# One attention product on 128 rows, a queue given to the scheduler, paired stores and a swapped copy in a fused attention and mixer kernel

## The chip, the cores and the metric

The kernel runs on one core of one Trainium2 chip. The metric is the device time of one execution in microseconds (us). The time before is 1947.83 us, the median of three runs (1947.3 to 1950.81).

## What is computed

Three layers in a row, on 8 batches of 576 tokens with 512 channels, all in 32-bit floats. Attention with keys and values averaged over eights, then a mixer with a low-rank product over tokens (U, V) and a two-layer network over channels, then a mixer that adds the real part of a two-dimensional Fourier transform, normalises, and applies a second two-layer network:

```python
k_p = k.reshape(B, H, Sp, pool, D).mean(axis=3)
v_p = v.reshape(B, H, Sp, pool, D).mean(axis=3)
scores = scale * np.matmul(q, k_p.transpose(0, 1, 3, 2))
scores = scores - np.max(scores, axis=-1, keepdims=True)
attn = np.exp(scores)
attn = attn / (np.sum(attn, axis=-1, keepdims=True) + 1e-09)
x = np.matmul(attn, v_p)                  # 8 heads side by side: 512 channels
u = x + (x.transpose(0, 2, 1) @ U @ V).transpose(0, 2, 1)
x = u + np.maximum(u @ w_ch1, 0.0) @ w_ch2
u = x + np.real(np.fft.fft(np.fft.fft(x, axis=1), axis=2))
un = (u - mu) / np.sqrt(var + 1e-06)
out = u + np.maximum(un @ w_ch1b, 0.0) @ w_ch2b
```

## The kernel before

Products run on TensorE in a reduced 32-bit format (`F32R`), with each operand split into a high and a low part, so that one product becomes three (high by high, high by low, low by high). Two of attention's products and its transposes run in plain 32-bit floats. The split takes a copy on ScalarE and a subtraction on VectorE or GpSimd (`split`, line 113).

**Attention** (`class Attn`, `tile_steps` from line 479) takes 128 tokens at a time: 5 tiles per batch, 40 in all. A tile's scores of 8 heads by 72 pooled keys make 576 columns. ScalarE exponentiates them head by head (line 503), TensorE transposes them (lines 507 to 509: four blocks of 128 columns, and one of 64 columns into `e1`), ScalarE copies the result into `e` (lines 512 and 513: a large copy of 512 columns and a small one of 64 partitions), and five products with `v` follow (lines 522 to 524). The fifth has 64 rows, for 576 is four and a half times 128. Tile `v` holds the averaged values with zeroes where a row belongs to another head. In the first batch three tiles are in flight, and three of its five tiles keep `e` in scratch space (`alt`); the other 37 tiles use the pool's `e`.

**Words.** The weights arrive as 64-bit floats and are converted to 32 bits by integer operations: `high` (a shift on VectorE, line 149, and an operation on ScalarE, line 150) and `bits` (two operations on VectorE, lines 154 and 155). `w_second` converts the second mixer's weights while attention is still running. Its second half takes 32 half words, each in one of two `cv` buffers, and stores each into the DRAM tensor `wd`; `w_swap` reads `wd` back much later.

**The last stage** (from line 1323, a loop over 14 blocks of 512 tokens, `seq`, 5 of the first mixer and 9 of the second; there are 13 changes of block). Each block runs 8 steps of 7 products (`product`, with weights combined beforehand, in the DRAM tensors `wc`), whose sums need fewer products than the plain way; between them stand the second layer's products of the step before (`st2_a`). A product is 12 matmuls. The combined weights come through a ring of four tiles `wr` of two products each (`ring_load`, line 971); 392 such loads of 512 KB run in the stage, and a tile is refilled one product after TensorE has finished with it. Around the products, four calls of `tick` per step advance the generators ("lanes") of the other work: attention's remaining tiles, the Fourier transform (`Dft`, loads `F` and `R` from `x1d`, stores to `u2d`), the preparation of the next block (`prep_a`, loads `ul`, statistics `mv`), `w_second`. At the end of a block the residuals `ur` are added and stored to `x1d` or `out` (line 1082), one per 128 tokens. In this stage attention runs in the way called `lean`: the small transpose goes into the right half of bank `h0`, whose left half is the target `u` of the products (`halves[0]`), and each step of a tile waits for its `tick`.

**What sets the order.** The program is written as a sequence; a scheduler orders each engine's instructions by a simulated timeline, except for engines named in a `manual_schedule` block, which keep the order of the program. ScalarE is named from the second group of blocks on, and in the last stage TensorE, VectorE and SyncE. SyncE issues nearly all DMAs, so its order is that of the transfers. The simulated timeline takes the place of times that the scheduler doesn't have; a queue whose head waits holds up all behind it. GpSimd is ordered by the scheduler throughout.

The lines that are touched:

```python
for c in range(4):
    nc.tensor.transpose(e0[:, c * 128:c * 128 + n], sf[:n, c * 128:c * 128 + 128], ident[:n, :n])
nc.tensor.transpose(e1[:64, :n], sf[:n, 512:S], ident[:n, :n])
...
k = TT[c][1]
mm(o[:n, h0 * D:(h0 + nh) * D], e[:k, c, :n], self.v[:k, v0:v0 + nh].rearrange("p h d -> p (h d)"), c == 0, c == 4)
```

Of the kernel before, what the change touches and what calls it, by code (L numbers as in the profile page):

```python
# [8 lines left out]
F32 = mybir.dt.float32  # L9
F32R = mybir.dt.float32r  # L10
I32 = mybir.dt.int32
ACTF = mybir.ActivationFunctionType
# [5 lines left out]
B, H, S, D = 8, 8, 576, 64  # L18
# [9 lines left out]
TT = [(0, 128), (128, 128), (256, 128), (384, 128), (512, 64)]  # L28
# [17 lines left out]
def kernel(  # L46
# [18 lines left out]
    nc = tc.nc  # L65
# [7 lines left out]
    ident = const.tile([128, 128], F32, name="ident")  # L73
# [6 lines left out]
    def scratch(i, w=1024, dt=F32):  # L80

        return wp.tile([128, w], dt, tag=f"w{i % 2}_{NF - 1 - i // 2}", name=f"scr{i}")
# [5 lines left out]
    wd = dram.tile([NF, 128, 512], F32, name="wd")  # L88
    wc = [dram.tile([7 * NPR, 128, 512], F32, name=f"wc{i}") for i in range(2)]

    def bank(tag):
        return ps_b.tile([128, 512], F32, tag=tag, name=tag)
# [9 lines left out]
    def at_tick(i):  # L102

        while state["lean"] and state["tick"] != i and not state["flush"]:
            yield

    def sub(eng, o, a, b):
        eng.tensor_tensor(out=o, in0=a, in1=b, op=ALU.subtract)  # L108
# [4 lines left out]
    def split(hi, lo, src, eng=None):  # L113
        nc.scalar.activation(out=hi, in_=src, func=ACTF.Copy)  # L114
        sub(eng or nc.vector, lo, src, hi.bitcast(F32))

    def mm(o, a, b, start, stop):
        nc.tensor.matmul(o, a, b, start=start, stop=stop, skip_group_check=True)  # L118
# [3 lines left out]
    def later(fn):  # L122

        if state["free"]:
            pend.append((state["clock"], fn))
        else:
            fn()
# [6 lines left out]
    def store(o, i):  # L134
        later(lambda: nc.sync.dma_start(out=o, in_=i))
# [6 lines left out]
    def pair(raw, n):  # L142
        v = raw.rearrange("p (n e) -> p n e", e=2)
        return v[:, 0:n, 0], v[:, 0:n, 1]

    def high(raw, n, t):

        lw, hw = pair(raw, n)
        nc.vector.tensor_scalar(out=t, in0=lw, scalar1=29, scalar2=None, op0=ALU.logical_shift_right)
        nc.scalar.activation(out=lw.bitcast(F32), in_=hw.bitcast(F32), func=ACTF.Abs, scale=F64_BIAS)  # L150

    def bits(raw, n, t):
        lw, hw = pair(raw, n)
        nc.vector.scalar_tensor_tensor(out=t, in0=hw, scalar=-0x80000000, in1=t, op0=ALU.bitwise_and, op1=ALU.bitwise_or)
        nc.vector.scalar_tensor_tensor(out=t, in0=lw, scalar=3, in1=t, op0=ALU.logical_shift_left, op1=ALU.bitwise_or)
        return t.bitcast(F32)
# [90 lines left out]
    def w_second(at):  # L247

        def load(src):
            raw = at.cv().bitcast(I32)  # L250
            nc.sync.dma_start(out=raw, in_=src.bitcast(I32))
            return raw

        def half(p, i, h):
            return w1b[2 * p + i][:, 256 * h:256 * h + 256]

        def raw_of(o):
            return o[:, 1].bitcast(F32)

        def put(o, n):  # L260
            split(o[:, 0], o[:, 1], raw_of(o), nc.gpsimd)
            store(wc[1][n], o.bitcast(F32).rearrange("p h x -> p (h x)"))

        n = [(p, i, h) for p in range(NPR) for i, h in ((0, 0), (1, 0), (1, 1), (0, 1))]
        ahead = [load(half(*n[0])), load(half(*n[1]))]
        at_n = [2]

        def word():
            raw = ahead.pop(0)
            o = at.wo()  # L270
            t = raw_of(o).bitcast(I32)
            high(raw, 256, t)
            yield
            bits(raw, 256, t)
            if at_n[0] < len(n):
                ahead.append(load(half(*n[at_n[0]])))
                at_n[0] += 1
            yield
            return o

        for p in range(NPR):
            z = 7 * p
            b11 = yield from word()
            b12 = yield from word()
            t1 = at.wo()
            sub(nc.vector, raw_of(t1), raw_of(b12), raw_of(b11))
            put(b11, z)
            yield
            b22 = yield from word()
            t2 = at.wo()  # L290
            sub(nc.vector, raw_of(t2), raw_of(b22), raw_of(t1))
            put(t1, z + 1)
            yield
            sub(nc.vector, raw_of(b12), raw_of(b22), raw_of(b12))
            put(b22, z + 4)
            yield
            put(b12, z + 3)
            b21 = yield from word()
            t4 = at.wo()
            sub(nc.vector, raw_of(t4), raw_of(b21), raw_of(t2))  # L300
            put(t2, z + 2)
            yield
            put(b21, z + 6)
            put(t4, z + 5)
            yield
        def load2(i):
            raw = at.wo().bitcast(I32).rearrange("p h x -> p (h x)")
            nc.sync.dma_start(out=raw, in_=w2b[i // 2][:, 256 * (i % 2):256 * (i % 2) + 256].bitcast(I32))
            return raw

        ahead = [load2(i) for i in range(3)]
        yield
        yield
        for i in range(2 * NF):
            raw = ahead.pop(0)
            t = at.cv()[:, 0:256].bitcast(I32)
            high(raw, 256, t)
            yield
            c = slice(256 * (i % 2), 256 * (i % 2) + 256)
            store(wd[i // 2][:, c], bits(raw, 256, t))  # L320
            if i + 3 < 2 * NF:
                ahead.append(load2(i + 3))
            yield
# [9 lines left out]
    class Attn:  # L333
        def __init__(self, c):
            p1 = self.p = c.enter_context(tc.tile_pool(name="at", bufs=1, side="right"))
            self.k = p1.tile([128, NPAIR, 2 * SP], F32, name="k")
            self.v = p1.tile([128, 12, D], F32, name="v")
            self.s = p1.tile([128, S], F32, name="s")
            self.mask = p1.tile([128, 12], F32, name="vmask")
            self.ust = p1.tile([128, 5, 4, RANK], F32R, name="ust")  # L340
            self.usf = scratch(21)[:, 0:20 * RANK].rearrange("p (t g r) -> p t g r", t=5, g=4)
            self.vst = p1.tile([128, S], F32R, name="vst")
            self.kp = {}
            self.hu = {}
            self.q = {}
            self.raw = {}
            self.mixing = False
            self.done = {}
            self.xq = [scratch(12 + t) for t in range(5)]
            self.x0 = [z[:, 0:512] for z in self.xq]  # L350

        def setup(self):
            nc.vector.memset(self.k, 0.0)
            nc.gpsimd.memset(self.usf[:, :, 1, :], 0.0)
            nc.gpsimd.dma_start(out=self.mask, in_=vmask)

        def tmp(self):
# [114 lines left out]
        def tile_steps(self, b, t, alt=0, before=None):  # L472
            p1 = self.p

            n = 128

            def banks():
                return [bank("soh"[alt] + i) for i in "01"]
# [3 lines left out]
            for p in range(NPAIR):  # L482
                o = sc[p // 2][:n, (p % 2) * 144:(p % 2) * 144 + 144]
# [5 lines left out]
            sf = scratch(3 + alt) if alt else self.s  # L489
# [3 lines left out]
            for i in range(2):  # L493
                h = slice(4 * i, 4 * i + 4)
# [9 lines left out]
            yield  # L504
            yield from at_tick(3)
            e0, e1 = (bank("s0"), halves[0][:, 256:512]) if state["lean"] else banks()
            for c in range(4):
                nc.tensor.transpose(e0[:, c * 128:c * 128 + n], sf[:n, c * 128:c * 128 + 128], ident[:n, :n])
            nc.tensor.transpose(e1[:64, :n], sf[:n, 512:S], ident[:n, :n])
            e = scratch(4 + 2 * alt, 640) if alt else p1.tile([128, 640], F32, tag="e", name="e")  # L510
            e = e.rearrange("p (c k) -> p c k", c=5)
            nc.scalar.activation(out=e[:, 0:4, :n], in_=e0.rearrange("p (c k) -> p c k", c=4)[:, :, :n], func=ACTF.Copy)
            nc.scalar.activation(out=e[:64, 4, :n], in_=e1[:64, :n], func=ACTF.Copy)
            nc.vector.tensor_scalar(out=sm[:n], in0=sm[:n], scalar1=1e-9, scalar2=None, op0=ALU.add)
            nc.vector.reciprocal(out=sm[:n], in_=sm[:n])
            yield
# [3 lines left out]
                    before()  # L520
            o = bank("soh"[alt] + "0")
            for c, (v0, h0, nh) in enumerate(VSLOT):
                k = TT[c][1]
                mm(o[:n, h0 * D:(h0 + nh) * D], e[:k, c, :n], self.v[:k, v0:v0 + nh].rearrange("p h d -> p (h d)"), c == 0, c == 4)
            if b == 0:
                xf = self.x0[t]
            else:
# [622 lines left out]
    at = Attn(abx)  # L1150
# [171 lines left out]

    prev, rows, low = None, None, None
    chain = ExitStack()
    chain.enter_context(tc.manual_schedule(engines={mybir.EngineType.PE, mybir.EngineType.DVE, mybir.EngineType.SP}))
    for k in range(len(seq)):
        begun = k + 1 == len(seq)
        for p in range(NPR):
            x = ops[k]
            n = 7 * (NPR * k + p)  # L1330
# [4 lines left out]
            h0, h1 = halves[0], bank("h1")  # L1335
# [153 lines left out]
```

## Time and profile before

| | before |
|---|---|
| median of three runs | 1947.83 us |
| the profiled execution | 1953.33 us |
| its span, first to last instruction | 1951.5 us |
| mean granted TensorE clock | 0.980 |
| TensorE matmuls busy | 1849.3 us (95%), 11500 instructions |
| TensorE weight loads busy | 1646.2 us (84%) |
| VectorE busy | 1070.6 us (55%) |
| ScalarE busy | 719.8 us (37%) |
| GpSimd busy | 197.2 us (10%) |
| moved by DMA | 423.78 MB, mean 217 GB/s |

The table comes from the page of the profiled execution. PE is TensorE's matmuls, PEld its weight loads, DVE VectorE, ACT ScalarE, POOL GpSimd, and SP SyncE; a "q" behind the name marks an instruction of the engine's queue, such as the issue of a DMA. L118 is a line of the kernel; as it belongs to the helper that issues every matmul, the names of the tiles tell products apart. Matmuls are pipelined and their ends are modelled, so starts tell more than durations. A group's mean is in nanoseconds, all else in microseconds. A wait is put down to the event that ended it.

### The profile page before, as it was taken

How to read it: one execution, taken by the hardware profiler on the slowest of the kernel's cores; microseconds unless marked ns; L12 is line 12 of the kernel's file. 1: busy time of each engine (PE TensorE's matmuls, PEld its weight loads, DVE VectorE, ACT ScalarE, POOL GpSimd, SP SyncE). 2: the span in 40 equal slices, each digit the busy share in tenths (PEclk: the TensorE clock that was granted, in tenths of full speed). 3: DMA queues.
4: the chain of work that ended last, by engine and by line, in shares of the span. 5: the costliest groups of instructions: out<-in, count | busy, mean ns of one | idle time of the engine just before them, and what ended most of it. 6: DMA issues, size and time to landing. Idle time of an engine off the chain costs nothing. (4 is left out here: it accounts for less than half of the span.)

```text
span 1951.5 us, 32024 instructions
## 1 busy us (share of the span) xinstructions
PE 1849.3 (95%) x11500; PEld 1646.2 (84%) x11500; DVE 1070.6 (55%) x2457; ACT 719.8 (37%) x2201; POOL 197.2 (10%) x335
## 2 busy tenths in 40 slices
PE   5789999999998998999999999999999999999999
PEld 4678888888887887898998888899989999999998
DVE  7884466656665554445455665555545544444332
ACT  5552444444454443333333433333323333232321
POOL 3440122221200000000001000100010000000000
PEclk8799999999999999999999999999999999999999
DMA  9654474757576677867576867676767666757664
GB/s 362 224 167 133 141 217 149 234 165 243 182 257 229 217 238 248 282 209 242 191 255 221 270 226 238 199 242 220 221 206 245 210 226 190 244 165 238 192 197 151
DMA packets 265278, 423.78 MB, mean 217 GB/s; under 512 B 45792, under 2 KB 76608, under 8 KB 265120
## 3 DMA queue, kind: packets, MB, share of 16 engines
q1 hardware_dynamic: 264192, 418.34, 66.3%
q0 software_dynamic: 928, 3.40, 0.5%
q8 instruction: 91, 1.49, 0.3%
q14 instruction: 67, 0.55, 0.1%
HBM read 342.09 MB, written 79.56 MB: 216 GB/s over the span
## 5 line engine op out<-in xcount | busy, mean ns | idle before, releaser
L118 PE MATMUL h<-x,wr 128*128 128x256 f32 x4704 | 646.4, 285 | 27.3 <-DMA wr<-wc 14.3
L118 PEld LDWEIGHTS h<-x,wr 128*128 128x128 f32 x4704 | 618.5, 192 | 62.1 <-issue 10.6
L118 PE MATMUL o<-w,hh 128*128 128x512 f32 x1312 | 371.7, 400 | 8.6 <-ACT hh L1026 5.9
L118 PEld LDWEIGHTS o<-w,hh 128*128 128x128 f32 x1312 | 228.3, 190 | 44.5 <-ACT hh L1026 9.1
L118 PEld LDWEIGHTS h<-utx,w 128*128 128x128 f32 x1536 | 203.4, 195 | 21.5 <-DVE hl L1027 9.6
L118 PE MATMUL h<-utx,w 128*128 128x256 f32 x1536 | 212.8, 290 | 9.1 <-DVE hl L1027 5.8
L111 DVE TENSOR_TENSOR side<-h,side 128x256 f32<-128x256 f32 x224 | 124.0, 553 | 172.9 <-PE h L118 171.6
L118 PE MATMUL o<-w,hl 128*128 128x512 f32 x656 | 212.0, 397 | 0.0
L1302 ACT ACTIVATE hh<-side 128x256 fp32r<-128x256 f32 x224 | 117.0, 522 | 146.6 <-DVE side L111 130.6
L1302 ACT ACTIVATE hh<-h 128x256 fp32r<-128x256 f32 x112 | 43.2, 386 | 300.1 <-PE h L118 298.5
L1308 DVE SCALAR_TENSOR_TENSOR hl<-h,hh 128x256 fp32r<-128x256 f32 x112 | 47.5, 424 | 181.1 <-ACT hh L1302 181.1
L1308 DVE SCALAR_TENSOR_TENSOR hl<-side,hh 128x256 fp32r<-128x256 f32 x224 | 123.4, 551 | 28.3 <-ACT hh L1302 28.2
L118 PEld LDWEIGHTS o<-w,hl 128*128 128x128 f32 x656 | 119.9, 190 | 22.0 <-DVE hl L1027 0.5
L118 PE MATMUL m<-w,hh 128*128 128x512 f32 x464 | 128.7, 398 | 0.0
L118 PE MATMUL hu<-w,hh 128*128 128x512 f32 x448 | 124.3, 400 | 0.0
L503 ACT ACTIVATE s<-s,mx 128x72 f32<-128x72 f32 x296 | 90.4, 329 | 43.4 <-DVE mx L496 43.1
L108 POOL TENSOR_TENSOR wo<-wo 128x256 fp32r<-128x256 f32 x88 | 68.9, 799 | 305.8 <-ACT wo L114 236.4
L108 DVE TENSOR_TENSOR x<-ul,x 128x256 fp32r<-128x256 f32 x182 | 70.1, 421 | 47.3 <-ACT x L114 47.2
L118 PEld LDWEIGHTS m<-w,hh 128*128 128x128 f32 x464 | 81.1, 192 | 11.0
L1349 ACT ACTIVATE side<-h 128x256 f32<-128x256 f32 x112 | 42.9, 383 | 120.3 <-PE h L118 119.9
L118 PEld LDWEIGHTS hu<-w,hh 128*128 128x128 f32 x448 | 78.2, 192 | 10.3
L118 PEld LDWEIGHTS s<-v,e 128*128 128x128 f32 (+1 forms) x370 | 59.5, 195 | 18.9 <-issue 9.0
(250 smaller groups left out, 2392.3 us busy)
## 6 DMA issues: line engine op xcount, KB each, us to landing
wr<-wc SPq DMA_DIRECT2D x392, 512.0 KB
wc<-wo SPq DMA_DIRECT2D x88, 256.0 KB
x<-x SPq DMA_DIRECT2D x56, 256.0 KB
ur<-ud SPq DMA_DIRECT2D x36, 256.0 KB
x1d<-ur SPq DMA_DIRECT2D x36, 256.0 KB
ul<-u2d SPq DMA_DIRECT2D x36, 256.0 KB
ur<-u2d SPq DMA_DIRECT2D x36, 256.0 KB
out<-ur SPq DMA_DIRECT2D x36, 256.0 KB
```

Source lines behind the costliest of these rows:

```text
L108: eng.tensor_tensor(out=o, in0=a, in1=b, op=ALU.subtract)
L111: eng.tensor_tensor(out=o, in0=a, in1=b, op=ALU.add)
L118: nc.tensor.matmul(o, a, b, start=start, stop=stop, skip_group_check=True)
L503: nc.scalar.activation(out=s[:n, a], in_=v[:, k], func=ACTF.Exp, bias=mx[:n, a:a + 1], accum_out=sm[:n, a:a + 1])
L1302: nc.scalar.activation(out=hh[:, i], in_=c, func=ACTF.Relu)
L1308: nc.vector.scalar_tensor_tensor(out=hl[:, i], in0=c, scalar=0.0, in1=hh[:, i].bitcast(F32), op0=ALU.max, op1=ALU.subtract)
L1349: nc.scalar.activation(out=sb, in_=v, func=ACTF.Copy)
```

## The change

It has four parts. The fifth product with `v` reads all 128 partitions of `e` and `v`; the upper halves are set to zero, once for the lasting tiles (`e` now lasts for the whole of attention) and per tile for scratch. The small transpose and the small copy stand ahead of the large ones. In `w_second` two converted half words share one `cv` buffer and leave with one store. In the last stage SyncE is no longer among the engines that keep the program's order.

```diff
@@ w_second
         for i in range(2 * NF):
             raw = ahead.pop(0)
-            t = at.cv()[:, 0:256].bitcast(I32)
+            if i % 2 == 0:
+                w = at.cv()
+            t = w[:, 256 * (i % 2):256 * (i % 2) + 256].bitcast(I32)
             high(raw, 256, t)
             yield
-            c = slice(256 * (i % 2), 256 * (i % 2) + 256)
-            store(wd[i // 2][:, c], bits(raw, 256, t))
+            bits(raw, 256, t)
+            if i % 2:
+                store(wd[i // 2], w)
@@ Attn.__init__
+            self.e = p1.tile([128, 640], F32, name="e")
@@ Attn.setup
+            nc.gpsimd.memset(self.v[64:128, 11], 0.0)
+            nc.gpsimd.memset(self.e[64:128, 512:640], 0.0)
@@ Attn.tile_steps
+            nc.tensor.transpose(e1[:64, :n], sf[:n, 512:S], ident[:n, :n])
             for c in range(4):
                 nc.tensor.transpose(e0[:, c * 128:c * 128 + n], sf[:n, c * 128:c * 128 + 128], ident[:n, :n])
-            nc.tensor.transpose(e1[:64, :n], sf[:n, 512:S], ident[:n, :n])
-            e = scratch(4 + 2 * alt, 640) if alt else p1.tile([128, 640], F32, tag="e", name="e")
+            e = scratch(4 + 2 * alt, 640) if alt else self.e
+            if alt:
+                nc.gpsimd.memset(e[64:128, 512:640], 0.0)
             e = e.rearrange("p (c k) -> p c k", c=5)
+            nc.scalar.activation(out=e[:64, 4, :n], in_=e1[:64, :n], func=ACTF.Copy)
             nc.scalar.activation(out=e[:, 0:4, :n], in_=e0.rearrange("p (c k) -> p c k", c=4)[:, :, :n], func=ACTF.Copy)
-            nc.scalar.activation(out=e[:64, 4, :n], in_=e1[:64, :n], func=ACTF.Copy)
...
-                k = TT[c][1]
-                mm(o[:n, h0 * D:(h0 + nh) * D], e[:k, c, :n], self.v[:k, v0:v0 + nh].rearrange("p h d -> p (h d)"), c == 0, c == 4)
+                mm(o[:n, h0 * D:(h0 + nh) * D], e[:, c, :n], self.v[:, v0:v0 + nh].rearrange("p h d -> p (h d)"), c == 0, c == 4)
@@ the last stage
-    chain.enter_context(tc.manual_schedule(engines={mybir.EngineType.PE, mybir.EngineType.DVE, mybir.EngineType.SP}))
+    chain.enter_context(tc.manual_schedule(engines={mybir.EngineType.PE, mybir.EngineType.DVE}))
```

## Rows read from the trace of the kernel before

**Rows 1.** Table of stretches: length, busy us (instructions) by engine, TensorE clock, DMA share, GB/s.

```profile
500.00:600.00 100.00, 92.20 (x587) 81.22 (x587) 65.20 (x162) 50.81 (x197) 14.43 (x21) 0.99 0.75 245
...
1600.00:1700.00 100.00, 100.00 (x632) 90.18 (x631) 47.52 (x114) 30.06 (x76) 4.05 (x6) 1.00 0.67 220
```

**Rows 2.** List of waits, TensorE: who, for whom, us in total, times, longest.

```profile
PE h L118 <- DMA wr<-wc: 14.3, 8, 2.7
...
PE h L923 <- DVE side L111: 6.5, 3, 5.7
...
PE h L118 <- ACT e L513: 6.2, 7, 1.8
...
PE h L118 <- DVE mv L892: 4.4, 1, 4.4
```

**Rows 3.** Groups by form: names, shapes, count | busy, mean ns | idle before, releasers.

```profile
L508 PE MATMUL s<-ident,s 128*128 128x128 f32 x148 | 26.6, 274 | 1.6 <-ACT s L503 1.3
...
L118 PEld LDWEIGHTS s<-v,e 64*128 64x128 f32 x74 | 11.1, 188 | 8.9 <-issue 8.6 <-ACT hh L1026 0.3
```

**Rows 4.** Timeline, 640 to 650 us: start, length, engine, instruction, count [idle before, releaser].

```profile
640.82 1.59 PE L118 MATMUL h<-x,wr 128*128 128x256 f32 x12
...
647.16 1.29 PEld L118 LDWEIGHTS s<-v,e 128*128 128x128 f32 x8
...
648.67 0.29 PEld L118 LDWEIGHTS s<-v,e 64*128 64x128 f32 x2 [0.23 <-issue]
...
649.03 1.48 PEld L118 LDWEIGHTS h<-x,wr 128*128 128x128 f32 x12
649.03 1.69 PE L118 MATMUL h<-x,wr 128*128 128x256 f32 x12
```

**Rows 5.** Timeline, the copies of one tile in the last stage, around 661 us.

```profile
660.81 0.58 ACT L512 ACTIVATE e<-s 128x512 f32<-128x512 f32 x1
...
661.28 0.26 ACT L513 ACTIVATE e<-h 64x128 f32<-64x128 f32 x1
...
661.60 0.62 PE L118 MATMUL h<-x,wr 128*128 128x256 f32 x3 [1.79 <-ACT e L513]
```

**Rows 6.** Timeline of GpSimd, a memset at the start.

```profile
3.44 0.26 POOL L354 MEMSET scr<- 128x160 f32 x1
```

**Rows 7.** Timeline around two stalls of VectorE, 598 and 740 us.

```profile
598.18 0.42 PE L509 MATMUL h<-ident,s 128*64 128x128 f32 x1 [3.93 <-DVE hl L1308]
...
732.17 0.42 SPq L135 DMA_DIRECT2D wd<-cv  x1
...
740.19 0.29 DVE L149 TENSOR_SCALAR cv<-wo 128x256 int32<-128x256 int32 x1 [7.02 <-DMA wd<-cv]
...
742.66 1.11 PE L923 MATMUL h<-ident,ul 128*128 128x128 f32 x4 [5.73 <-DVE side L111]
```

**Rows 8.** Table of stretches of 4 us around the two stalls.

```profile
734.00:738.00 4.00, 2.93 (x19) 2.29 (x17) 0.00 (x0) 0.00 (x0) 0.00 (x0) 1.00 1.02 313
742.00:746.00 4.00, 3.34 (x13) 3.15 (x14) 2.08 (x5) 2.13 (x5) 0.00 (x0) 0.50 0.68 233
...
598.00:602.00 4.00, 3.08 (x12) 2.38 (x13) 2.03 (x6) 1.75 (x4) 0.00 (x0) 0.50 0.66 242
```

**Rows 9.** List of waits of SyncE's queue, whole kernel.

```profile
SPq L971 <- PE h L118: 614.7, 278, 7.1
SPq L1082 <- DVE ur L111: 95.3, 36, 12.4
```

**Rows 10.** Timeline of SyncE and TensorE around a change of block, 1098 to 1125 us.

```profile
1098.40 4.84 SPq L971 DMA_DIRECT2D wr<-wc  x3
...
1113.18 0.38 SPq L971 DMA_DIRECT2D wr<-wc  x1
...
1124.61 1.67 PE L118 MATMUL h<-x,wr 128*128 128x256 f32 x12 [2.64 <-DMA wr<-wc]
```

**Rows 11.** Timeline of SyncE, four residual loads at a change of block.

```profile
799.19 4.63 SPq L1062 DMA_DIRECT2D ur<-ud  x4
```

## Prediction

> **What bounds the kernel now.** I read the table of stretches first. The reader is to see the TensorE column: in the late stretch it is busy for all of the 100 us, while in the attention stretch 7.8 us of 100 are missing [rows 1]. So TensorE's queue is the bound throughout, and a change can win in two ways only: by taking time off TensorE's own instructions, or by closing one of the gaps in it. Then I read the list of waits for TensorE. In the last stage, the chain of seven products, the gaps have few owners: a ring load of combined weights that lands late (14.3 us in 8 waits), VectorE's `side` (6.5 us), the small copy L513 (6.2 us in 7 waits), and the statistics `mv` (4.4 us in one) [rows 2]. Late in that stage there is nothing left to close [rows 1]. The profiled execution took 1953.33 us with a span of 1951.5; the median of the three runs is 1947.83, 5.5 us less. I make the sum in the profile's microseconds and take it off the median, because no term below is larger than a few tens of us and 0.3% of it is nothing.
>
> **Part 1, the fifth product on 128 rows.** Before, the last of five products of a tile of attention reads 64 partitions, with two weight loads of 64 rows. They cost no more than full ones (188 ns mean), but they have an idle stretch ahead of them: 8.9 us over 74 loads, 8.6 of it held by nothing that the profile shows [rows 3]. In the timeline it is plain: eight full weight loads end at 647.16 + 1.29 = 648.45, the 64-row pair begins at 648.67 after 0.23 us of idle weight path, ends at 648.96, and the next product's loads begin at 649.03, 0.07 later [rows 4]. All other weight loads there follow without a gap, so full-row loads should too. Saved per tile: 0.23 + 0.07 = 0.30 us. The lower end is 0.23 (entering alone); the upper is 0.40, since the next product's twelve matmuls then also took 1.69 us against 1.59 elsewhere [rows 4]. I take 0.30, because both gaps stand in the row and the 0.10 may be the modelled ends. There are 40 tiles (37 in `e`, 3 in scratch): 12 us, ends 9.2 and 16. The Trainium skill, "TensorEngine Tiling (Array Packing)", section Key Properties, says that a change of tiling mode drains TensorE; the row agrees for the way in, with 0.23 us, and by that rule, which holds for the way in and out, the sum is the 12 us, and by the way in alone 9.2. Not all of it reaches the end: the attention stretch has 7.8% of gaps that other engines set, and time saved ahead of such a gap only widens it. I count three quarters: **9 us**.
>
> What it adds: zeroes for the upper halves of `e` and `v`, two memsets at the start and three for the scratch tiles of the first batch, all on GpSimd. A larger one there took 0.26 us [rows 6]. Nothing waits for them but the fifth product of a tile, which comes after four others and two copies, so I cost them at nothing; without that cover they are at most 5 x 0.26 = 1.3 us.
>
> **Part 2, small transpose and small copy first.** In the last stage of attention (`lean`) the small transpose shares a bank with TensorE's next product. So that product waits for L513, which stands behind the large copy L512: they start at 660.81 and 661.28, and TensorE starts at 661.60 after 1.79 us [rows 5]. Swapped, L513 starts where L512 starts now, 0.47 us earlier, and TensorE with it. Seven tiles: 7 x 0.47 = 3.3 us; TensorE waits in all seven [rows 2], so I take **3 us**. What is late next is ScalarE's queue ahead of L512, which keeps the rest of the 1.79. Two waits are moved ahead of work that did not wait for them: the four large transposes (26.6 us over 37 tiles, 0.72 us each [rows 3]) now queue behind the small one, which needs the last exponential and, in `lean`, VectorE's `hl` (3.93 us at 598.18 [rows 7]). Where that wait binds, up to 0.72 us of transposes follow it instead of preceding it; in `lean` TensorE then stands waiting for ScalarE anyway, which covers it. Without that cover it is 7 x 0.72 = 5 us. Ends: 3.3 gained, 2 lost.
>
> **Part 3, two converted words in one buffer and one store.** `w_second` puts one converted half word into each of two `cv` buffers, and VectorE's order is fixed by hand. So when a `cv` store has not landed, the next conversion stops VectorE, and all behind it: at 740.19 after 7.02 us, for a store of which SyncE shows the issue at 732.17; TensorE's transposes at 742.66, which wait for `side` behind it, lost 5.73 us. At 598.18 the same happened with 3.93 us, behind `hl` [rows 7]. After each, the granted clock stood at 0.50 for the next stretch of 4 us [rows 8], the lower of its two levels (1.2 of 2.4 GHz), which costs up to 2.0 us each. With two words per buffer, a conversion waits for the store of the pair before the last, so two to three words old instead of one to two. The two stalls then go: 5.7 + 3.9 + 4.0 = 13.6 us. What is late next is the ring: the DMA engines are full in 734 to 738 (share 1.02 [rows 8]), so a TensorE that doesn't stop there may soon wait for weights. I count two thirds: **9 us**; ends 0 and 13.6. Sixteen stores fewer save SyncE 16 x 0.42 us (the issue at 732.17), which I cost at nothing, since SyncE stands waiting for most of that stage [rows 9].
>
> **Part 4, SyncE in the scheduler's order.** In the last stage SyncE issues in program order and stands behind whatever comes first: 614.7 us behind TensorE for ring loads, 95.3 us behind VectorE for the residual stores, the longest 12.4 [rows 9]. The first costs nothing by itself. The second does: at each end of a block SyncE stops at loads and stores of the block's end, and then issues everything at once. Around 1100 us the ring loads end at 1098.40 + 4.84, the next is issued at 1113.18, ten microseconds later, and at 1124.61 TensorE waits 2.64 us for one [rows 10]. A queue ordered by a simulated time puts what is ready ahead of what is not; moved past each other are the ring loads (392), the block loads `ul`, `ur`, `F`, `R`, and the stores `x1d`, `u2d` and `out`. At most it closes the waits for ring loads and for `mv`: 14.3 + 4.4 = 18.7 us [rows 2]. No row shows how well the simulated times fit the chip here, so the other end is a loss (the last rival). I take half, nearest to the rows in which SyncE demonstrably stood still: **9 us**.
>
> Sum: 9 + 3 + 9 + 9 = 30; 1947.8 - 30 = **1918 us**.
>
> **Rivals.**
> 1. *SyncE's new order gains nothing.* For it: full DMA engines (1.02), not only the order, delay ring loads. Against: the ten idle microseconds [rows 10]. Then 9 + 3 + 9 = 21 are left: 1927 us.
> 2. *The stall on `cv` is replaced by a wait for ring loads* at the same places, since the transfers' backlog stays. For it: the same 1.02. Against: four ring tiles stand ahead. Then 9 + 3 + 9 = 21: also 1927 us.
> 3. *Nothing reaches the end*: the saved matmul time and the closed stalls are taken up by ScalarE and VectorE in the stage where attention runs. For it: the 7.8 us of gaps in the attention stretch; against: TensorE is busy for the other 92. About 1946 us.
> 4. *Slower: block loads overtake ring loads.* The simulated order lets block loads out as soon as their buffers are free, so that they lie ahead of the ring loads that TensorE needs next. The place is each of the 13 changes of block in the last stage. The trace has one such case in little: four `ur` loads held SyncE for 4.63 us at 799.19 [rows 11], and a wait for the ring followed, of the longest kind (2.7 [rows 2]). With two such waits at each of 13 changes, 13 x 5.4 = 70 us, less the 14 that are there: 56 lost, 21 gained by the rest, 1947.8 + 35 = 1983 us. It decides from (21 + 14) / 13 = 2.7 us at each change, one such wait. Against it: late changes show none, so there is slack in the ring. The Trainium skill, "DMA: Bandwidth & Descriptors", section Queues, rings and completion order, says that on each DMA engine descriptors are consumed in ring order; by that rule what SyncE issues early is also served early, which is this rival. The wait behind the four `ur` loads agrees.
>
> **How the numbers follow.** The forecast has 0.45, rivals 1 and 2 0.20 and 0.12, rival 3 0.10, rival 4 0.13. The largest gain is 16 + 3.3 + 13.6 + 18.7 = 52 us, 1896; the three middle rivals lie below 1948. The range 1897 to 1948 leaves out rival 4 and a little on either side. A measurement of this kernel tells about 0.2% (3.9 us) from no change. Faster takes the forecast, rivals 1 and 2 and a fifth of rival 3: 0.79. Same takes most of rival 3: 0.08. Slower is rival 4: 0.13.
>
> **What would show it.** Part 1: no idle ahead of the fifth product's weight loads, and no 64-row form. Part 2: no wait of TensorE for L513, and less before the next product. Part 3: no DVE wait for `wd` stores; the gaps at 598 and 742 gone and the clock at 1.0 there. Part 4: fewer waits of TensorE for `wr`, ring loads issued at even distances across a change of block. The prediction is wrong if ring waits grow in number at the changes of block, or if the stretches before the last stage, where the simulation orders all queues anew, come out longer by more than part 1 gives.

## The result, and the profile after

The changed kernel takes 1916.13 us, the median of four runs (1915.26 to 1920.1), beside 1949.32 us (1947.3 to 1952.44) for the kernel before. The ratio is 0.9832, with an interval of 0.9812 to 0.9853, so about 33 us are gone. The forecast was 1918 us. The sum of 30 us was nearly right, yet three of its four terms were not: done alone, the parts give about 9, 0, 3 and 24 where the prediction had 9, 3, 9 and 9.

From the page of the changed kernel, its span and the busy time of TensorE (matmuls and weight loads), VectorE, ScalarE and GpSimd; the execution took 1916.54 us:

```profile
span 1914.8 us, 31951 instructions
...
PE 1827.1 (95%) x11500; PEld 1638.3 (86%) x11500; DVE 1074.9 (56%) x2457; ACT 717.8 (37%) x2201; POOL 194.5 (10%) x340
```

The span is 36.7 us shorter. TensorE's busy time falls from 1849.3 to 1827.1 us, so 22.2 us are matmuls that took less time, and the other 14.5 are gaps that closed. The prediction thought mostly of gaps.

The table of stretches of the changed kernel, with the columns of [rows 1]; the first two lines answer to [rows 1], the third to the last line of [rows 8]:

```profile
500.00:600.00 100.00, 92.03 (x597) 82.30 (x596) 67.61 (x165) 51.71 (x200) 14.28 (x21) 0.99 0.72 238
1600.00:1700.00 100.00, 100.00 (x634) 90.18 (x633) 43.02 (x105) 29.74 (x74) 2.58 (x4) 1.00 0.70 201
598.00:602.00 4.00, 3.80 (x18) 3.22 (x17) 1.65 (x5) 2.47 (x7) 0.00 (x0) 0.57 1.07 378
```

Nothing moved in the attention stretch or late in the last stage. What changed lies in the last stage's first 840 us: its last wait of over 1 us ended at 1419 us before. The granted clock at 598 us is still low (0.57, where the prediction wanted 1.0), but TensorE is busy for 3.80 us of the 4 where it was busy for 3.08.

The list of waits of the changed kernel, for TensorE and then for VectorE (for whom, us in total, times, longest):

```profile
PE h L118 <- DMA wr<-wc: 4.1, 4, 2.0
PE h L513 <- DVE hl L1315: 2.6, 2, 2.0
...
PE h L118 <- DVE side L111: 2.2, 4, 0.8
...
PE h L118 <- ACT e L520: 1.6, 2, 0.9
...
PE h L930 <- DVE side L111: 0.5, 2, 0.3
...
DVE cv L149 <- DMA wd<-cv: 0.6, 1, 0.6
```

All owners of [rows 2] have shrunk: the ring from 14.3 to 4.1 us, the small copy (now L520) from 6.2 to 1.6, the wait of 4.4 us for `mv` is gone, and the transposes' wait for `side` (now L930) fell from 6.5 to 0.5. The products' own wait for `side` grew a little, to 2.2 us in short waits (1.2 before). For `hl` TensorE still waits 2.6 us at the place of the stall at 598 us, where it waited 3.9.

To compare kernels by stage, two lines were read from the view of each tile: the first product of attention's stage (`h<-utx`) and the first of the last stage (`h<-x,wr`), with shortest, median and longest duration in ns, first start and last start. For the changed kernel:

```profile
L118 PE MATMUL h<-utx,w x1536: 274/283/582, 71.6 to 583.3; 128*128 128x256 f32 x192
L118 PE MATMUL h<-x,wr x4704: 274/283/583, 585.3 to 1903.9; 128*128 128x256 f32 x196
```

and for the kernel before:

```profile
L118 PE MATMUL h<-utx,w x1536: 274/283/582, 68.9 to 580.2; 128*128 128x256 f32 x192
L118 PE MATMUL h<-x,wr x4704: 274/283/583, 582.1 to 1940.7; 128*128 128x256 f32 x196
```

So the start stage lasts to 71.6 us (68.9 before), attention's stage 585.3 - 71.6 = 513.7 us (513.2), and the last stage, to the end of the span, 1914.8 - 585.3 = 1329.5 us (1369.4). The whole gain, 39.9 us, lies in the last stage, and 2.7 us of it were lost again at the start. The table of stretches tells gaps from slower matmuls in that stage; the first line is the kernel before, the second the changed one:

```profile
582.10:1951.50 1369.40, 1326.24 (x8335) 1192.21 (x8333) 688.96 (x1638) 448.57 (x1199) 57.43 (x166) 0.99 0.69 222
585.30:1914.80 1329.50, 1311.71 (x8335) 1184.67 (x8333) 687.78 (x1637) 446.76 (x1199) 58.28 (x166) 1.00 0.72 229
```

TensorE is idle for 43.2 us of it before and for 17.8 after, so 25.4 of the 39.9 us are gaps and 14.5 are matmul time. All kernels side by side, times in us:

| kernel | median | ratio to before, interval | start | attention | last stage |
|---|---|---|---|---|---|
| before | 1949.32 | | 68.9 | 513.2 | 1369.4 |
| changed | 1916.13 | 0.9832, 0.9812 to 0.9853 | 71.6 | 513.7 | 1329.5 |
| e1_rows_alone | 1941.75 | 0.9956, 0.9940 to 0.9972 | 68.2 | 512.2 | 1366.1 |
| e2_small_first | 1950.27 | 1.0009, 0.9992 to 1.0026 | 71.4 | 517.9 | 1363.6 |
| e3_pairs_alone | 1945.88 | 0.9984, 0.9963 to 1.0005 | 68.7 | 520.0 | 1357.9 |
| e4_sync_alone | 1928.49 | 0.9879, 0.9845 to 0.9913 | 68.7 | 517.9 | 1338.8 |
| e5_all_but_rows | 1921.90 | 0.9857, 0.9835 to 0.9879 | 70.7 | 518.1 | 1330.6 |
| e6_all_but_small_first | 1917.21 | 0.9830, 0.9807 to 0.9854 | 69.2 | 510.4 | 1333.2 |
| e7_all_but_pairs | 1918.37 | 0.9834, 0.9806 to 0.9861 | 71.7 | 510.9 | 1336.3 |
| e8_store_later | 1949.10 | 1.0004, 0.9987 to 1.0021 | 68.8 | 518.9 | 1368.9 |
| e9_small_first_late_only | 1915.42 | 0.9826, 0.9801 to 0.9851 | 68.5 | 514.3 | 1329.5 |
| e10_changed_again | 1919.04 | 0.9844, 0.9817 to 0.9871 | 72.1 | 515.1 | 1333.7 |
| e11_stores_elsewhere | 1949.54 | 1.0005, 0.9983 to 1.0026 | 69.1 | 510.6 | 1368.0 |
| e12_loads_elsewhere | 1941.29 | 0.9958, 0.9941 to 0.9975 | 68.8 | 513.2 | 1356.1 |

The stages come from one profiled execution each; those of e1, e2 and e8 are the longest of their ten runs. In before, e4, e8, e11 and e12, TensorE, VectorE and ScalarE execute the same instructions in the same order, and yet the middle column runs from 510.6 to 518.9. It can't be used for differences of a few us. The last column is steadier, but the changed kernel itself has 1329.5 and, taken again in e10, 1333.7. The verdicts rest on the medians.

### The profile page after: what moved, and what is told of

It is laid out like the page before. It is cut to its first block, busy times and chain, and to the rows that moved or that the text cites. A ratio compares the mean times of both kernels' runs of the same rounds, so it can differ in the third digit from the quotient of the medians.

```text
span 1914.8 us, 31951 instructions
## 1 busy us (share of the span) xinstructions
PE 1827.1 (95%) x11500; PEld 1638.3 (86%) x11500; DVE 1074.9 (56%) x2457; ACT 717.8 (37%) x2201; POOL 194.5 (10%) x340
## 3 DMA queue, kind: packets, MB, share of 16 engines
q1 hardware_dynamic: 261888, 418.33, 68.7%
## 5 line engine op out<-in xcount | busy, mean ns | idle before, releaser
L108 POOL TENSOR_TENSOR wo<-wo 128x256 fp32r<-128x256 f32 x88 | 68.5, 795 | 299.6 <-ACT wo L114 242.9
L118 PEld LDWEIGHTS m<-w,hh 128*128 128x128 f32 x464 | 80.2, 190 | 10.8
L118 PE MATMUL m<-w,hl 128*128 128x512 f32 x232 | 72.6, 391 | 0.0
```

## The experiments

The theory was the prediction's: four independent gains. The rivals were those of the prediction. First each part was done alone.

### Part 1 alone

```diff
...
-            e = scratch(4 + 2 * alt, 640) if alt else p1.tile([128, 640], F32, tag="e", name="e")
+            e = scratch(4 + 2 * alt, 640) if alt else self.e
...
-                mm(o[...], e[:k, c, :n], self.v[:k, v0:v0 + nh]..., c == 0, c == 4)
+                mm(o[...], e[:, c, :n], self.v[:, v0:v0 + nh]..., c == 0, c == 4)
```

> The kernel before with part 1 alone: the fifth product on 128 rows, with its zeroes. All expect the idle weight path ahead of that product to be gone, 0.30 us or a little more per tile in the starts. The prediction (three quarters of 12 us reach the end): 9 us faster. Rival (the attention stage before the last one is held by what the other engines hand over, so that the time saved there widens the next gap): only the 8 tiles of the last stage count, 8 x 0.34 = 2.7 us faster, and the start of the last stage stays within 2 us of 582.

It measured 1 - 0.9956 = 0.44%, 8.6 us (5.5 to 11.7), so the rival's 2.7 us fall. Its other sign, a start of the last stage within 2 us of 582, did come (580.4), but in a column that spreads by more than that: in which stage the 8.6 us were saved isn't shown. In the groups by form the fifth product, 16.2 us in 74 matmuls at 300 ns before, has become (count | busy, mean ns | idle before):

```profile
L118 PE MATMUL s<-v,e 128*128 128x64 f32 x74 | 12.6, 253 | 0.0
```

The timeline of the changed kernel, to be held beside [rows 4] (start, length, engine, instruction, count):

```profile
643.80 1.61 PEld L118 LDWEIGHTS s<-v,e 128*128 128x128 f32 x10
644.02 1.53 PE L118 MATMUL s<-v,e 128*128 128x128 f32 x10
...
645.33 1.50 PEld L118 LDWEIGHTS h<-x,wr 128*128 128x128 f32 x12
```

All ten weight loads now stand in one row, without idle time ahead of the last two. From the first of them to the first load of the next product it is 645.33 - 643.80 = 1.53 us, where [rows 4] have 649.03 - 647.16 = 1.87. The switch to 64 rows and back cost 0.34 us per tile. In e1, with part 1 alone, the median of the same distance is 1.54 us over 22 tiles that can be read in both, beside 1.88 in the kernel before.

### Part 2 alone

```diff
+            nc.tensor.transpose(e1[:64, :n], sf[:n, 512:S], ident[:n, :n])
             for c in range(4):
                 nc.tensor.transpose(e0[...], ...)
-            nc.tensor.transpose(e1[:64, :n], sf[:n, 512:S], ident[:n, :n])
...
+            nc.scalar.activation(out=e[:64, 4, :n], in_=e1[:64, :n], func=ACTF.Copy)
             nc.scalar.activation(out=e[:, 0:4, :n], ...)
-            nc.scalar.activation(out=e[:64, 4, :n], in_=e1[:64, :n], func=ACTF.Copy)
```

> The kernel before with part 2 alone: the small transpose and the small copy first. The prediction: 3 us faster, all of it in the seven tiles of the last stage, where TensorE's wait for the small copy shrinks by 0.47 us each. Rival (the large transposes now queue behind VectorE's hl and the last exponential): no change or up to 2 us slower.

It measured no change: 1.8 us slower, between 1.6 faster and 5.1 slower. That is what its rival said. The wait that it aims at did shrink, in the list of waits for TensorE, from 6.2 us in 7 [rows 2] to

```profile
PE h L118 <- ACT e L512: 2.0, 3, 0.9
```

The last stage is 5.8 us shorter in the table, but the start stage is longer. This holds for every kernel: with part 2 for all tiles (changed, e2, e5, e7, e10) the start stage ends between 70.7 and 72.1 us, mean 71.5; without it there, in the nine others, between 68.2 and 69.2, mean 68.8. The timeline of TensorE in the changed kernel shows where the 2.7 us go (in brackets: idle time before, and what ended it):

```profile
39.45 2.08 PE L118 MATMUL hu<-scr,scr 128*128 128x512 f32 x2 [5.56 <-DVE scr L536]
...
58.95 0.80 PE L118 MATMUL o<-hst,vst 128*128 128x512 f32 x1 [6.97 <-DVE hst L108]
```

and in the kernel before:

```profile
45.13 2.08 PE L118 MATMUL hu<-scr,scr 128*128 128x512 f32 x2 [2.92 <-DVE scr L529]
...
57.58 0.79 PE L118 MATMUL o<-hst,vst 128*128 128x512 f32 x1 [2.59 <-DVE hst L108]
```

In the first batch three tiles are in flight and the scheduler orders the engines. With the swap it orders them otherwise, and TensorE waits for VectorE for longer: over the start, 9.3 us for `scr` and 7.0 for `hst`, beside 6.4 and 2.6 before.

### Part 3 alone

```diff
-            t = at.cv()[:, 0:256].bitcast(I32)
+            if i % 2 == 0:
+                w = at.cv()
+            t = w[:, 256 * (i % 2):256 * (i % 2) + 256].bitcast(I32)
...
-            store(wd[i // 2][:, c], bits(raw, 256, t))
+            bits(raw, 256, t)
+            if i % 2:
+                store(wd[i // 2], w)
```

> The kernel before with part 3 alone: two converted words in one buffer and one store. The prediction: the stalls of 3.9 and 5.7 us at 598 and 740 and the half clock behind them go, 9 us faster (at most 13.6). Rival (the wait for ring loads takes their place, as the DMA engines are full there): 0 to 3 us faster, with new waits for wr between 735 and 760.

It measured 3.1 us, with an interval from 7.2 gained to 1.0 lost. The list of waits, for TensorE and VectorE:

```profile
PE h L118 <- DMA wr<-wc: 14.2, 7, 3.9
...
PE h L926 <- DVE side L111: 0.9, 2, 0.6
...
DVE cv L149 <- DMA wd<-cv: 0.7, 1, 0.7
```

The wait for `wd` stores was 17.3 us in 7 in the kernel before and is gone, the transposes' wait for `side` fell from 6.5 [rows 2] to 0.9, and the ring waits are what they were, 14.2 beside 14.3. Of new ring waits between 735 and 760 us, the rival's sign, there is one of 0.8 us. The last stage is 11.5 us shorter in the table. The time shows less than that, and lies at the edge of the rival's 0 to 3 us. A part is lost just ahead of the last stage, where the conversions begin. There TensorE now waits for `hl`:

```profile
563.38 2.93 PE L118 MATMUL h<-utx,w 128*128 128x256 f32 x12 [3.40 <-DVE hl L1030]
```

A wait of 1.7 to 4.5 us for this `hl` stands between 553 and 564 us in all six kernels with part 3 (changed, e3, e5, e6, e9, e10), and in none of the eight without it. The rest of the difference isn't explained.

### Part 4 alone

```diff
-    chain.enter_context(tc.manual_schedule(engines={mybir.EngineType.PE, mybir.EngineType.DVE, mybir.EngineType.SP}))
+    chain.enter_context(tc.manual_schedule(engines={mybir.EngineType.PE, mybir.EngineType.DVE}))
```

> The kernel before with part 4 alone: SyncE in the scheduler's order in the last stage. The prediction: 9 us faster, from the waits for ring loads at the changes of block and for mv. Rival A (the order also issues the wd stores earlier, and so closes the two stalls that part 3 is meant to close): 18 us or more faster, and part 3 is then worth little beside it. Rival B (ring loads overtaken by block loads): slower, with more waits for wr than the 8 of before.

It measured 23.6 us (17.0 to 30.2), the largest part of the change by far. It is also the cleanest experiment: the other four engines execute the same instructions in the same order as before, and SyncE's order differs only from the start of the last stage on.

The waits of this kernel, for TensorE, VectorE, and SyncE's queue:

```profile
PE h L118 <- DMA wr<-wc: 2.0, 2, 1.8
...
PE h L923 <- DVE side L111: 0.8, 2, 0.5
...
DVE cv L149 <- DMA wd<-cv: 12.7, 8, 5.1
...
SPq L971 <- PE h L118: 651.3, 307, 6.6
SPq L1082 <- DVE ur L111: 19.9, 10, 14.4
```

The ring waits went from 14.3 to 2.0, `side` from 6.5 to 0.8, `mv` from 4.4 to nothing: 12.3 + 5.7 + 4.4 = 22.4 us of gaps. The first holds in every profile: 14.2 to 17.3 us in the six kernels where SyncE keeps the program's order and all its loads (before, e1, e2, e3, e8, e11), 2.0 to 5.0 in the seven with part 4. The wait for `mv`, at 1419 us, has counterparts of 2.8 to 5.1 us within 9 us of that time in e1, e2, e3, e8 and e11; most are put down to the ring, so one wait seems to stand there under several names. In e4 there is none. SyncE stands behind VectorE's residuals for 19.9 us instead of 95.3 [rows 9]. What it does instead is in its timeline at the same change of block as [rows 10]:

```profile
1095.84 0.37 SPq L971 DMA_DIRECT2D wr<-wc  x1
1096.31 1.72 SPq L644 DMA_DIRECT2D F<-x1d  x2
...
1103.17 0.82 SPq L1082 DMA_DIRECT2D x1d<-ur  x2
1104.08 0.40 SPq L971 DMA_DIRECT2D wr<-wc  x1
...
1105.68 0.43 SPq L971 DMA_DIRECT2D wr<-wc  x1
...
1108.35 0.37 SPq L971 DMA_DIRECT2D wr<-wc  x1
```

The residual stores, the `F` and `R` loads and the ring loads alternate. From the end of one ring issue to the end of the next, over 7.5 us pass 24 times in the 392 issues of the kernel before, the longest 12.6 us, and 8 times here, the longest 8.9. One long distance is left in these lines: 1104.48 - 1096.21 = 8.3 us.

The clock comes on top of the gaps. The last stage of this kernel, to be held beside the first line of the same table under the result:

```profile
586.60:1925.40 1338.80, 1315.81 (x8335) 1185.25 (x8333) 688.42 (x1638) 447.90 (x1199) 57.68 (x166) 1.00 0.72 227
```

It is 30.6 us shorter: 43.2 - 23.0 = 20.2 us of gaps, and 1326.24 - 1315.81 = 10.4 us off the same 8335 matmuls. In e8 and e11, which are no faster than the kernel before, these matmuls take 1327.8 and 1324.7. One block of the kernel before:

```profile
711.40:815.70 104.30, 94.85 (x563) 84.15 (x564) 48.80 (x109) 29.60 (x74) 3.03 (x7) 0.95 0.79 253
```

the same block with SyncE in the scheduler's order, and the two places of [rows 8] between 734 and 746:

```profile
715.00:808.50 93.50, 90.72 (x563) 80.62 (x564) 48.65 (x109) 29.70 (x74) 3.02 (x7) 1.00 0.84 282
734.00:738.00 4.00, 4.00 (x28) 3.66 (x27) 1.69 (x5) 0.44 (x1) 0.00 (x0) 1.00 1.06 395
742.00:746.00 4.00, 4.00 (x26) 3.58 (x25) 1.73 (x5) 1.76 (x6) 0.00 (x0) 1.00 0.74 247
```

Of 10.8 us, gaps give (104.30 - 94.85) - (93.50 - 90.72) = 6.7, and the same 563 matmuls, at a granted clock of 1.00 for 0.95, give 94.85 - 90.72 = 4.1. The stall at 740 us is gone though the DMA engines are just as full (1.06). The one at 598 us stays, so of rival A the time came (18 us or more) and one of its two stalls. It has 4.49 us ahead of TensorE:

```profile
603.71 0.42 PE L509 MATMUL h<-ident,s 128*64 128x128 f32 x1 [4.49 <-DMA wo<-w2b]
```

### Each of three parts undone

The changed kernel without one part. e5 undoes part 1, e6 part 2, e7 part 3, each with the lines above turned round, for e7:

```diff
-            if i % 2 == 0:
-                w = at.cv()
-            t = w[:, 256 * (i % 2):256 * (i % 2) + 256].bitcast(I32)
+            t = at.cv()[:, 0:256].bitcast(I32)
...
-            if i % 2:
-                store(wd[i // 2], w)
+            store(wd[i // 2][:, c], bits(raw, 256, t))
```

> The changed kernel with part 1 undone (64-row product again). If part 1 is worth beside the others what it is worth alone (0.44%, some 8.6 us): 1924 to 1925 us, 1.2 to 1.3% under the kernel before. Rival (what part 1 saves is taken up by the stage before the last one, and its gain alone came from another ordering of that stage): within 3 us of the changed kernel, 1.5 to 1.7% under the kernel before.

> The changed kernel with part 2 undone. Prediction: 3 us slower than the changed kernel, 1.5% under the kernel before. Rival (as alone, where it was worth 0.1% the other way, within its interval): no difference to the changed kernel, or a little faster, 1.7 to 1.8% under the kernel before. In the last stage the wait of TensorE for the small copy returns, some 6 us over seven tiles.

> The changed kernel with part 3 undone (each converted word in its own buffer and store). Rival A (SyncE's order had closed most of what part 3 was to close): within 3 us of the changed kernel, 1.5 to 1.7% under the kernel before. Prediction (9 us for part 3, independent of part 4): 1925 us, 1.2% under. In the trace: if VectorE's waits for the wd store stay under 5 us in sum, the order is what closed them; if a stall of over 3 us at 598 or 740 returns, part 3 is needed beside it.

The changed kernel itself was timed twice, at 0.9832 and 0.9844 (e10). Against these, part 1 is worth 2.5 to 4.9 us beside the others, part 2 costs 0.4 to 2.7, and part 3 is between 0.4 gained and 1.9 lost. Each ratio has an interval of 0.2 to 0.3%, some 4 to 6 us, to either side: none of the three can be told from nothing, nor part 1 from its 8.6 alone. e5 lies between its two forecasts; e6 is as its rival said, though TensorE's wait for the small copy is back (5.2 us in 6). In e7 the stall on `cv` is back, and TensorE waits for `hl` behind it. The lists of waits, for VectorE and TensorE:

```profile
DVE cv L149 <- DMA wd<-cv: 17.6, 9, 4.9
...
PE h L510 <- DVE hl L1312: 6.2, 2, 5.6
```

So by the trace part 3 is needed to close that gap, yet by the medians undoing it costs 0.4 us at most, which is rival A's forecast; the last stage, 1336.3, is 2.6 or 6.8 us longer than in the two profiles of the changed kernel.

### What in SyncE's order it was

Three runs on the kernel before. The prediction had blamed the residual stores, so e8 puts them one call of `tick` later, and e11 issues them from GpSimd:

```diff
@@ e8
-            nc.sync.dma_start(out=(x1d, out)[phase][r0:r0 + 128, :], in_=r)
+            store((x1d, out)[phase][r0:r0 + 128, :], r)
...
+    clock()
@@ e11
-            nc.sync.dma_start(out=(x1d, out)[phase][r0:r0 + 128, :], in_=r)
+            nc.gpsimd.dma_start(out=(x1d, out)[phase][r0:r0 + 128, :], in_=r)
```

> The kernel before, SyncE in the program's order, with one edit: the stores of the residual sums at a block's end are issued one tick later in the program instead of at once, so that SyncE does not stand at them while VectorE has not added yet. The same work is done. If standing behind these stores (95 us in the kernel before) is what starves the ring at a change of block: 5 to 12 us faster than the kernel before, fewer than 8 waits for wr. Rival (the block loads F, R and ul, and their own waits ahead of ring loads, are what starves it): no change, within 3 us, the waits for wr stay at 14 us.

e8 measured no change (24 distances of over 7.5 us, as before), but the edit didn't remove the wait, which now stands in line 135, where `store` issues; so it says nothing on the stores. From its list of waits of SyncE's queue:

```profile
SPq L135 <- DVE ur L111: 96.9, 47, 12.4
```

> The kernel before, SyncE in the program's order, with the residual stores at a block's end issued from GpSimd's queue instead of SyncE's, so that SyncE cannot stand at them. The same work is done. If standing at these stores (95 us of SyncE's waits) keeps ring loads back: fewer than 15 distances of over 7.5 us between ring loads (24 before) and 8 us or more faster. Rival (the loads F, R, ul and ur ahead of them do): 20 or more such distances, within 4 us of the kernel before.

In e11 the wait of 95.3 us in line 1082 is gone from SyncE, and the time is the same: 1.0005, 0.9983 to 1.0026. TensorE's ring waits are not fewer, and 29 distances between ring loads are over 7.5 us, where fewer than 15 were expected. The list of waits, for TensorE and SyncE's queue:

```profile
PE h L118 <- DMA wr<-wc: 16.8, 8, 5.1
...
SPq L873 <- DMA out<-ur: 27.8, 6, 6.9
...
SPq L873 <- DMA x1d<-ur: 8.2, 2, 4.6
```

Some of the standing has moved to the block loads `ul` (line 873), which now wait 36.0 us for the stores to land and free their buffers (4.2 before). So the wait for the residual stores by itself isn't what makes ring loads late. But the equal time doesn't show that this wait costs nothing. TensorE's last matmuls and the last store, first in the kernel before, then in e11:

```profile
1944.48 4.41 SPq L1082 DMA_DIRECT2D out<-ur  x4
1947.18 0.61 PE L118 MATMUL o<-w,hl 128*128 128x512 f32 x2
...
1939.33 0.61 PE L118 MATMUL o<-w,hl 128*128 128x512 f32 x2
1940.97 0.54 POOL L1082 DMA_DIRECT2D out<-ur  x1 [0.82 <-DVE ur L111]
```

From the end of the last matmul to the end of the span it is 1951.5 - 1947.8 = 3.7 us before and 1947.7 - 1939.9 = 7.8 in e11, whose last stores leave from GpSimd. From the start of the last stage to that matmul it is 1365.7 us before, 1365.2 in e8, and 1360.3 in e11. So in one profile some 5 us were gained, and 4 of them lost again at the end. GpSimd, which now stands at the stores of `out` for 427.6 us in all, may hold up its other work besides.

e12 leaves the stores on SyncE and lets GpSimd issue the block loads `ul` of the blocks after the first, and `ur`:

```diff
-            nc.sync.dma_start(out=us[t], in_=(ud, u2d)[phase][r0:r0 + 128, :])
+            (nc.gpsimd if len(pools) > 1 else nc.sync).dma_start(out=us[t], in_=(ud, u2d)[phase][r0:r0 + 128, :])
...
-        nc.sync.dma_start(out=res["a", t], in_=(ud, u2d)[phase][r0:r0 + 128, :])
+        nc.gpsimd.dma_start(out=res["a", t], in_=(ud, u2d)[phase][r0:r0 + 128, :])
```

> The kernel before, SyncE in the program's order, with the block loads ul and ur of the last stage issued from GpSimd's queue. The same work is done. If the program's place of these loads, with their waits for free buffers, keeps ring loads back: fewer than 15 distances of over 7.5 us between ring loads, the waits for wr under 8 us, and 8 us or more faster. Rival (the stores, or F and R, do): 20 or more such distances, within 4 us of the kernel before; or slower, if the issues on GpSimd hold up its own work.

It gains 8.2 us (4.9 to 11.5), a third of part 4, while SyncE stands longer than ever behind the stores. The lists of waits, for SyncE's queue and TensorE:

```profile
SPq L1082 <- DVE ur L111: 120.4, 46, 14.4
...
PE h L118 <- DMA wr<-wc: 9.8, 6, 4.9
```

Of the three signs that were asked for, the time alone came. The ring waits fell to 9.8 us, not under 8, and 21 distances are over 7.5 us, which is the rival's sign. What did go are four waits of the kernel before: at 925, 1030, 1227 and 1419 us (2.2 + 1.7 + 2.4 + 4.4 = 10.7 us) e12 has none of over 1 us, while the one at 808 us grew from 2.7 to 4.9 and one of 1.7 is new at 896. So the block loads' place on SyncE's queue is one cause, by the time; how they delay the ring is argued. What the other two thirds are was not tried. What is left are the residual stores (by e11's profile some 5 us) and the loads and stores of the lanes (`F`, `R`, `wo`, `wd`), which stand between the ring loads in [rows 10]; that it is the latter isn't shown.

### Part 2 in the last stage alone

```diff
-            nc.tensor.transpose(e1[:64, :n], sf[:n, 512:S], ident[:n, :n])
+            if state["lean"]:
+                nc.tensor.transpose(e1[:64, :n], sf[:n, 512:S], ident[:n, :n])
             for c in range(4):
                 nc.tensor.transpose(e0[...], ...)
+            if not state["lean"]:
+                nc.tensor.transpose(e1[:64, :n], sf[:n, 512:S], ident[:n, :n])
...
```

and the two copies likewise, on the changed kernel.

> The changed kernel with the small transpose and copy first in the last stage alone, and last in the stages before it. Theory (the swap gains 3 us where the bank is shared and costs 2 to 3 us at the start, where the first use of the weights came at 71 us with the swap and at 68 to 69 without): start at 68.2 to 69.2 us, and 2 to 3 us faster than the changed kernel, 1.8 to 1.9% under the kernel before. Rival (the start differs by chance of the schedule): start at 71 us, no difference to the changed kernel.

> The changed kernel itself, beside the one with the swap in the last stage alone. Both theories: 1.6 to 1.8% under the kernel before, start at 71 to 72 us.

On one chip, e9 took 1915.42 us (1912.34 to 1917.76, five runs) and the changed kernel 1919.04 (1915.14 to 1922.63). That is 3.6 us less, but the ranges and the intervals overlap, and e6, without the swap, has the same ratio within 0.04%: which of them is best can't be told. It is 1.7% under the kernel before, a little short of the 1.8 to 1.9 that were forecast. Its start stage ends at 68.5 us, as the theory said, and its wait for the small copy is as short as in e2:

```profile
PE h L118 <- ACT e L524: 1.8, 3, 0.9
```

## Why the prediction was right and wrong

**The total** was right by errors that cancelled, which is luck: alone, the parts measure 8.6 - 1.8 + 3.1 + 23.6 = 33.5 us, beside 33 together. That they add up isn't shown by this: undone one at a time, parts 1 to 3 are by the medians worth 4.9 us together at most, beside 9.9 alone, and part 4 was not undone.

**Part 1** was right in mechanism and, done alone, in size: 9 forecast, 8.6 measured. Beside the others it may be worth less (2.5 to 4.9 in e5). The price of 0.30 us per tile measured 0.34. The Trainium skill, "TensorEngine Tiling (Array Packing)", section Key Properties, says that a change of tiling mode drains TensorE. The trace agrees: the way in and out cost 0.34 us.

**Part 2** had the right wait and nearly the right size for the last stage (the wait fell from 6.2 to 2.0, 4.2 for 3 forecast). The step that failed is its scope: it was priced over the seven tiles in `lean`, and the swap also touches the tiles of the start, whose stage grew by 2.7 us. What is lost there isn't the transposes' wait that the prediction priced, but longer waits for VectorE's `scr` and `hst`.

**Part 3** had the right mechanism: done alone, the stall of 5.7 us goes and that of 3.9 shrinks to 0.7, without the ring wait of rival 2 in their place. The term was sized too high, 3.1 for 9. Two steps of it failed. The 4.0 us for the clock hardly came: where the stall at 598 us was, the granted clock still falls (0.58 from 604 to 608 us in e3), and the matmuls of e3's last stage take 1324.0 us, 2.2 less than before and hardly outside what they take in before, e8 and e11 (1324.7 to 1327.8). And nothing was put down for the new order ahead of the last stage, which costs 3.4 us of waiting for `hl`. How the rest of the 11.5 us became 3.1 in the time stays open. Beside part 4 the term shrinks further, for 5.7 of its 13.6 us go with part 4 too: the stretches of e4 between 734 and 746 have no gap. One stall was counted in one part alone.

**Part 4** measured 23.6 for 9. Three steps of it failed. Half of the ring and `mv` waits was taken, where 12.3 + 4.4 = 16.7 of 18.7 went. `side` (5.7) was counted elsewhere. And the clock, priced in part 3 after each stall, was left out here: the matmuls of the last stage took 10.4 us less. With the 20.2 us of gaps that is the 30.6 us by which this stage is shorter in the profile; the time shows 23.6 (17.0 to 30.2). The blocker was misnamed as well: "The second does" was said of SyncE's wait for the residual stores, and with that wait taken away ring waits and time stayed as they were (e11).

**Rivals.** Rival 1 falls with e4. Rival 2's mechanism falls with e3, whose ring waits are 14.2 us beside 14.3, though its price, nothing gained by part 3, lies inside e3's interval. Rival 3 falls: time saved reaches the end. Rival 4, the slower one, loses from one ring wait at each of 13 changes of block; e4 has 2 in all and the changed kernel 4, so it falls. That block loads ahead of ring loads cost time seems true, but of the order before (e12).

## What to carry to other kernels

The long wait at the head of a queue need not be what delays the bound engine: issue the suspect from another queue, one kind at a time, and see which of that engine's waits go, and what the move costs where the work now leaves from. Price every gap of TensorE with the slower matmuls behind it, and a stall that two parts of a change both remove once. Where an edit is meant for one stage, apply it in that stage alone, since elsewhere it lets the scheduler order everything anew.

## What was not expected of the hardware

A gap costs more than its length. In the block from 711 us, 6.7 us of gaps came with 4.1 us of slower matmuls, at a granted clock of 0.95 for 1.00; over the last stage part 4 took 10.4 us off the same 8335 matmuls, beside 20.2 us of gaps.

One order of instructions on three engines gave 510.6 to 518.9 us for the same stage of 3020 matmuls, in five kernels. A single profile can't show a difference of a few us there.
